# A fixed order for ScalarE's work in the attention start of a three-layer kernel, with a ring of its own for one set of tables

## The chip, the cores and the metric

The kernel runs on one core of a Trainium2 chip. What counts is the device time of one execution in microseconds; the time of a kernel is the median of its runs. A profile is one further execution, recorded by the hardware profiler, with a time of its own. The engines are TensorE (PE, its weight loads PEld), VectorE (DVE), ScalarE (ACT), GpSimd (POOL) and SyncE (SP), which here only issues DMAs. Each engine takes its instructions in the order of its queue.

## The reference

Three layers follow one another. The first is a linear attention with a decaying state, for 4 sequences, 8 heads, 768 steps and 64 columns a head:

```python
for t in range(S):
    state = gamma * state + einsum('bhd,bhe->bhde', k[:, :, t], v[:, :, t])
    y[:, :, t] = scale * einsum('bhd,bhde->bhe', q[:, :, t], state)
```

Its result is taken as 3072 tokens of 512 columns. The second layer is `h = x @ w_in` (512 to 2048), `g = h - tanh(h)`, `g @ w_out` (2048 to 512). The third is `h = x @ w_in` (512 to 1024), a softmax weighting `h * softmax(h)`, a layer norm with the gain `g_ln`, and `@ w_out` (1024 to 512). The weights of both come as 64-bit numbers. All of it is in float32; the kernel splits each operand of the large products into a high and a low part and takes three products for one.

## The kernel before

**Units.** The attention is cut into 6 chunks of 128 steps for each of 4 sequences: 24 units, four for each chunk c; unit k belongs to chunk k // 4. `unit(ko, ks)` (lines 237 to 309) does the output of unit `ko` and then the scores of unit `ks`. For the output: small products "out" of the state and of the masked scores on TensorE (line 207), copies of the results out of PSUM by ScalarE (lines 272 to 276; in chunk 0 there are three, later two), an addition on VectorE (line 278), and in `split_x` the high parts by ScalarE (line 316) and the low parts by VectorE or GpSimd (line 317). For the scores: products "sc" of k with q and of k with v (line 207), the mask on VectorE (line 298), and the running state `sb`, which ScalarE copies in chunk 0 (line 304) and VectorE adds later (line 306). An output needs the masked scores and `sb` of its unit. I write sc(k) and out(k) for the two sets of products: 64 matmuls for sc, 48 (chunk 0) or 64 for out.

**Before a unit.** `prepare(k)` (lines 210 to 235) scales q by a table on GpSimd (line 220) and v by a column of constants, on ScalarE head by head (line 227) and, for `own < H` heads, the rest on GpSimd (line 231). For units 0 to 7 ScalarE has four of the eight heads, and the results lie in tiles of the kind "vq"; for units 8 to 11 it has all eight.

**Weights.** A decoder takes a weight tile through four stages: load of the raw words (line 115), Abs on ScalarE (line 121), four operations on VectorE (lines 128 to 136), and the high part on ScalarE and low part on VectorE (lines 144 and 145). `dec1.to(st, n)` brings stage `st` up to weight n.

**Second layer.** A step (n, b) is `products_h(b, n)`, twelve matmuls of 128x512 (line 329), a tanh on ScalarE (line 335) and a subtraction on VectorE (line 336); b is the block of 512 tokens, n the weight. Steps (0,0) and (1,0) are traced among units 4 to 7, the other thirty in the loop over n behind them; that loop also traces units 8 to 11, one for each n from 3 to 7, behind the two steps of its n. The `w_out` products y for these two blocks follow ("y products", line 353), fed by splits gh and gl of the results (lines 341 and 344). Later blocks run step by step to 750 us, then comes the third layer.

**Memory.** Tiles of 4 KB a partition come from a pool of 44 ("t4"), those of 2 KB from a pool of 17 ("t2"); q's tables, one for each chunk, are t2 tiles too.

**Order.** A scheduler puts each engine's instructions in order by a timeline of its own. Instructions may so leave the order in which the program traces them, unless `keep_in_program_order` ties one behind the instruction traced before it on its engine. Before, only the products of line 207 are tied; the matmuls of line 329, ScalarE's work and the DMAs are not. SyncE issues all loads named here.

Of the kernel before, what the change touches and what calls it, by code (L numbers as in the profile page):

```python
# [26 lines left out]
F32 = mybir.dt.float32  # L27
# [8 lines left out]
B, H, S, D = 4, 8, 768, 64  # L36
P = 128
DM = H * D
NT = B * S
NP = H // 2  # L40
# [5 lines left out]
NF1, NF2, NK = FF1 // P, FF2 // P, DM // P  # L46
# [1 line left out]
LAG = 2  # L48
LATER = 3
LOADS = 3  # L50
N4, N2 = 44, 17


W_MIN, W_MAX = (
# [7 lines left out]
C_IDENT = C_MASK + D  # L62
# [28 lines left out]
def body(ctx: ExitStack, tc, z, w_in, w_out, w_in2, w_out2, g_ln, cst, tab, out):  # L91
    nc = tc.nc
# [3 lines left out]
    mid = ctx.enter_context(tc.tile_pool(name="mid", bufs=N2))  # L96
    stp = ctx.enter_context(tc.tile_pool(name="stp", bufs=B + 2))
    yd = ctx.enter_context(tc.tile_pool(name="yd", bufs=1, space=DRAM))

    def t4(shape, dtype, name):  # L100
        return big.tile(shape, dtype, tag="t4", name=name)

    def t2(shape, dtype, name):
        return mid.tile(shape, dtype, tag="t2", name=name)
# [76 lines left out]
    loaded = [0]  # L181

    def load_tab(c):
        tb[c] = t2([P, NP * P], F32, "tab")
        nc.sync.dma_start(out=tb[c], in_=tab[c])

    def load_half(k, half):
        t = t4([P, 2, NP, P], F32, "z")
# [12 lines left out]
    def rows(h):  # L201
        return slice(h * D, (h + 1) * D)

    def products(todo):
        for o, a, b in todo:
            tc.keep_in_program_order(
                nc.tensor.matmul(o, a, b, start=True, stop=True, skip_group_check=True)  # L207
            )

    def prepare(k, own, wide=False):  # L210

        c = k // B
        if wide:
            t = t4([P, 2, H * D], F32, "vq")
            v = t[:, 0, :].rearrange("q (h d) -> q h d", h=H)
            qs[k] = t[:, 1, :].rearrange("q (p t) -> q p t", p=NP)
        else:
            v = t2([P, H, D], F32, "vs")
            qs[k] = t2([P, NP, P], F32, "qs")
        nc.gpsimd.tensor_tensor(  # L220
            qs[k].rearrange("q p t -> q (p t)"),
            zq[k][:, 0, :, :].rearrange("q p t -> q (p t)"), tb[c], ALU.mult,
        )
        src = zv[k][:, 1, :, :].rearrange("q p (h d) -> q (p h) d", h=2)
        c0 = C_VS + c * H
        for h in range(own):
            nc.scalar.activation(  # L227
                v[:, h, :], src[:, h, :], AF.Copy, scale=con[:, c0 + h : c0 + h + 1]
            )
        if own < H:  # L230
            nc.gpsimd.tensor_tensor(
                v[:, own:, :], src[:, own:, :],
                con[:, c0 + own : c0 + H].unsqueeze(2).to_broadcast([P, H - own, D]), ALU.mult,
            )
        vs[k] = v

    def unit(ko, ks, hold=False, pool=ps_r, tag="r", engs=None):


        if ko is not None:  # L240
            c, b = divmod(ko, B)
# [27 lines left out]
            ya = [t.rearrange("q h i t -> q (h i) t") for t in y]  # L269
            if c:  # L270
                for h in range(2):
                    nc.scalar.copy(xf[:, h, :, :], fr[h])
            else:
                for h in range(2):
                    nc.scalar.copy(xf[:, h, :, rows(1)], fr[h][:, :, rows(1)])
                nc.scalar.copy(xa[:, :, rows(0)], ya[0])
            for ab in steps:
                nc.vector.tensor_tensor(
                    xa[:, :, rows(ab)], xa[:, :, rows(ab)], ya[ab], ALU.add
                )  # L280
            if not hold:
                split_x(c, b, xf, engs or (nc.gpsimd, nc.gpsimd))
        if ks is not None:
            c = ks // B
            kt, kv, v, q = zq.pop(ks)[:, 1, :, :], zv.pop(ks), vs[ks], qs[ks]
# [22 lines left out]
                sa[ks + B] = stp.tile([P, NP, D], F32, tag="sa", name="sa")  # L308
                nc.vector.tensor_tensor(sa[ks + B], sb[ks], gn[1], ALU.add)

    def split_x(c, b, xf, engs):
        if b == 0:
            xt[c] = [[t4([P, 2, SB], F32R, f"x{n}") for _ in range(2)] for n in "hl"]
        for h in range(2):
            xh, xl = (xt[c][n][h][:, :, b * P : (b + 1) * P] for n in range(2))
            nc.scalar.copy(xh, xf[:, h, :, :])
            engs[h].tensor_tensor(xl, xf[:, h, :, :], xh.bitcast(F32), ALU.subtract)  # L317


# [2 lines left out]
    def products_h(s, f, pool, tag):  # L322
        ph = pool.tile([P, SB], F32, tag=tag, name="ph")
        (ah, al) = (w.rearrange("p (k c) -> p k c", k=NK) for w in dec1.w[f])
        n = 0
        for k in range(NK):
            xh, xl = (xt[s][m][k // 2][:, k % 2, :] for m in range(2))
            for a, x in ((ah, xh), (ah, xl), (al, xh)):
                nc.tensor.matmul(ph, a[:, k, :], x, start=n == 0, stop=n == 3 * NK - 1)  # L329
                n += 1  # L330
        return ph

# [71 lines left out]

    load_half(0, 0)
    load_tab(0)
    nc.sync.dma_start(out=con, in_=cst[:, :C_IDENT])
    load_half(0, 1)
    loaded[0] = 1
    load_units(3)  # L410
# [1 line left out]
    load_units(6)  # L412
    dec1.to(0, 2)
    load_units(2 * B)
    prepare(0, H // 2, True)
    prepare(1, H // 2, True)
    unit(None, 0, **spare)
    prepare(2, H // 2, True)
    unit(None, 1, **spare)
    for k in range(2 * B):  # L420
        if k + 3 < 2 * B:
            prepare(k + 3, H // 2, True)
        both = (nc.vector, nc.gpsimd) if k < 2 * B - 1 else (nc.vector, nc.vector)
        unit(k, k + 2 if k + 2 < 2 * B else None, engs=both, **spare)

        if k in (1, 4):
            for st in (1, 2):
                dec1.to(st, 1 + (k > 1))
        elif k in (2, 5):
            dec1.to(3, 1 + (k > 2))  # L430
        if k in (4, 6):
            step_h((k - 4) // 2, 0)
    dec1.to(0, 4)
    nc.sync.dma_start(out=gl, in_=g_ln)
    for n in range(NF1):
        while dec1.at[3] < n + 1:
# [240 lines left out]
```

## Time and profile before

| | us |
|---|---|
| median of 3 runs | 920.63 |
| their spread | 919.2 to 920.88 |
| the profiled execution | 919.89 |
| its span, first to last instruction | 918.1 |
| TensorE busy in the span | 878.7 (96%) |
| VectorE, ScalarE, GpSimd busy | 432.4, 300.5, 192.3 |

The span is 1.79 us shorter than the time of the same execution. Busy time of TensorE holds pipelined matmuls whose ends are modelled, so a full stretch may still run at a lower clock; the granted clock of a stretch (1.00 is the upper of its two levels, 2.4 GHz, 0.50 the lower, 1.2 GHz) is read beside it. In the rows, "idle before <- releaser" tells what ended an engine's wait; "issue" means that nothing in the profile explains it. A row "x4" merges four like instructions.

### The profile page before, as it was taken

How to read it: one execution, taken by the hardware profiler on the slowest of the kernel's cores; microseconds unless marked ns; L12 is line 12 of the kernel's file. 1: busy time of each engine (PE TensorE's matmuls, PEld its weight loads, DVE VectorE, ACT ScalarE, POOL GpSimd, SP SyncE). 2: the span in 40 equal slices, each digit the busy share in tenths (PEclk: the TensorE clock that was granted, in tenths of full speed). 3: DMA queues.
4: the chain of work that ended last, by engine and by line, in shares of the span. 5: the costliest groups of instructions: out<-in, count | busy, mean ns of one | idle time of the engine just before them, and what ended most of it. 6: DMA issues, size and time to landing. Idle time of an engine off the chain costs nothing.

```text
span 918.1 us, 15885 instructions
## 1 busy us (share of the span) xinstructions
PE 878.7 (96%) x6656; PEld 725.5 (79%) x6656; DVE 432.4 (47%) x873; ACT 300.5 (33%) x606; POOL 192.3 (21%) x200
## 2 busy tenths in 40 slices
PE   3669899999999999999999999999999999999998
PEld 3558688788888887888878888888888888888886
DVE  1664886995132323222222249973644444444442
ACT  3444543663111111111111133532533333333332
POOL 3511000000034433333333310010211222222210
PEclk9799999999999999999999999999999999999999
DMA  9750211532311113001311026205111111000000
GB/s 359 291 216 26 86 32 35 194 92 92 87 63 47 54 58 132 10 39 58 93 46 48 24 84 199 85 11 152 33 46 46 46 46 47 24 24 24 24 24 35
DMA packets 34775, 71.93 MB, mean 78 GB/s; under 512 B 3088, under 2 KB 15504, under 8 KB 34704
## 3 DMA queue, kind: packets, MB, share of 16 engines
q1 hardware_dynamic: 18576, 58.33, 18.9%
q10 hardware_dynamic: 16128, 12.59, 4.3%
q8 instruction: 52, 0.85, 0.4%
q14 instruction: 19, 0.16, 0.0%
HBM read 58.32 MB, written 12.58 MB: 77 GB/s over the span
## 4 chain that ended last, share of the span: by engine, by line
PE 92%; DMA 3%; ACT 1%; DVE 1%; issue 1%; SPq 1%; POOL 1%; ACTq 0%; POOLq 0%; DVEq 0%
PE py L353 28%; PE ph L329 28%; PE po L601 14%; PE ph L553 14%; PE out L207 3%; PE sc L207 2%; PE ptr L588 2%; DMA z<-z 1%; DMA raw<-w_in 1%; DMA y1d<-ysb 1%; SPq L189 0%; ACT vq L227 0%; POOL qs L220 0%; DVE wf L135 0%; ACT th L335 0%
## 5 line engine op out<-in xcount | busy, mean ns | idle before, releaser
L329 PE MATMUL ph<-xh,w 128*128 128x512 f32 x768 | 250.2, 395 | 7.7 <-ACT w L144 5.5
L353 PE MATMUL py<-gh,w 128*128 128x512 f32 x768 | 248.9, 392 | 1.2 <-ACT gh L341 1.2
L329 PEld LDWEIGHTS ph<-xh,w 128*128 128x128 f32 x768 | 146.3, 191 | 39.5 <-ACT w L144 5.9
L353 PEld LDWEIGHTS py<-gh,w 128*128 128x128 f32 x768 | 143.4, 188 | 31.9 <-ACT gh L341 1.6
L336 DVE TENSOR_TENSOR g<-ph,th 128x512 f32<-128x512 f32 x96 | 66.2, 689 | 183.7 <-ACT th L335 180.5
L329 PE MATMUL ph<-xl,w 128*128 128x512 f32 x384 | 151.7, 395 | 0.3 <-DVE xl L317 0.3
L353 PE MATMUL py<-gl,w 128*128 128x512 f32 x384 | 149.8, 390 | 0.0
L335 ACT ACTIVATE th<-ph 128x512 f32<-128x512 f32 x96 | 57.1, 597 | 266.6 <-PE ph L329 251.0
L553 PE MATMUL ph<-w,y 128*128 128x512 f32 x576 | 134.9, 389 | 0.0
L344 POOL TENSOR_TENSOR gl<-g,gh 128x512 fp32r<-128x512 f32 x48 | 61.7, 1286 | 346.3 <-DVE gh L343 332.3
L553 PEld LDWEIGHTS ph<-w,y 128*128 128x128 f32 x576 | 108.0, 188 | 22.4
L601 PE MATMUL po<-w,uh 128*128 128x512 f32 x384 | 120.4, 395 | 0.0
L388 POOL TENSOR_TENSOR y<-yl,y 128x512 fp32r<-128x512 f32 x24 | 42.2, 1760 | 260.9 <-ACT y L387 260.9
L329 PEld LDWEIGHTS ph<-xl,w 128*128 128x128 f32 x384 | 73.4, 191 | 15.8 <-DVE xl L317 0.7
L559 DVE TENSOR_REDUCE nmx<-ph 128x1 f32<-128x1024 f32 x24 | 29.4, 1225 | 117.7 <-PE ph L553 117.7
L353 PEld LDWEIGHTS py<-gl,w 128*128 128x128 f32 x384 | 72.1, 188 | 14.9
L601 PEld LDWEIGHTS po<-w,uh 128*128 128x128 f32 x384 | 70.5, 188 | 13.6
L601 PE MATMUL po<-w,ul 128*128 128x512 f32 x192 | 75.3, 392 | 0.0
L562 ACT ACTIVATE ex<-ph,nmx 128x1024 f32<-128x1024 f32 x24 | 26.8, 1117 | 132.5 <-DVE nmx L559 132.5
L564 DVE SCALAR_TENSOR_TENSOR ex<-ph,ex 128x1024 f32<-128x1024 f32 x24 | 29.4, 1225 | 29.8 <-ACT ex L562 29.8
L601 PEld LDWEIGHTS po<-w,ul 128*128 128x128 f32 x192 | 36.0, 188 | 7.6
L298 DVE TENSOR_TENSOR pr<-sc,con 128x256 f32<-128x256 f32 x48 | 19.8, 419 | 44.4 <-PE sc L207 44.4
(76 smaller groups left out, 849.3 us busy)
## 6 DMA issues: line engine op xcount, KB each, us to landing
z<-z SPq DMA_DIRECT2D x48, 512.0 KB, 5.2
raw<-w_in SPq DMA_DIRECT2D x24, 512.0 KB, 4.3
raw<-w_out SPq DMA_DIRECT2D x24, 512.0 KB, 3.6
y1d<-ysb ACTq DMA_DIRECT2D x24, 256.0 KB, 3.7
yl<-y1d SPq DMA_DIRECT2D x24, 256.0 KB, 3.2
out<-ob ACTq DMA_DIRECT2D x24, 256.0 KB, 2.2
tab<-tab SPq DMA_DIRECT2D x6, 256.0 KB, 3.8
ident<-cst SPq DMA_DIRECT2D x1, 64.0 KB, 8.1
```

What stands on the lines that cost most here:

```text
L207: nc.tensor.matmul(o, a, b, start=True, stop=True, skip_group_check=True)
L329: nc.tensor.matmul(ph, a[:, k, :], x, start=n == 0, stop=n == 3 * NK - 1)
L335: nc.scalar.activation(th, ph, AF.Tanh)
L336: nc.vector.tensor_tensor(g, ph, th, ALU.subtract)
L344: eng_l.tensor_tensor(gl_, g, gh.bitcast(F32), ALU.subtract)
L353: nc.tensor.matmul(py[e], a[:, cols], x, start=f == 0 and n == 0, stop=f == NF1 - 1 and n == 2)
L388: nc.gpsimd.tensor_tensor(yo, t, yh.bitcast(F32), ALU.subtract)
L553: nc.tensor.matmul(ph[:, half, :], a[:, k, :], b, start=n == 0, stop=n == 3 * NK - 1)
L559: nc.vector.tensor_reduce(nmx, phf, AX.X, ALU.max, negate=True)
L562: nc.scalar.activation(ex, phf, AF.Exp, bias=nmx, scale=1.0, accum_out=ssum)
L564: nc.vector.scalar_tensor_tensor(ex, phf, 1.0, ex, ALU.mult, ALU.mult, accum_out=us)
L601: nc.tensor.matmul(po, a[:, f, :], b, start=n == 0, stop=n == 3 * NF2 - 1)
```

## The change

The change has five parts:

- A helper `pin` ties an instruction in program order when asked. For units 0 to 7 it ties ScalarE's copies out of PSUM, its v scaling (`prepare` with `wide`) and its high parts. `prepare(k + 3)` moves from ahead of `unit(k, k + 2)` into it, between the copies and the additions (`amid`). At the start, `prepare` and `unit` of units 0 and 1 alternate.
- The matmuls of line 329 are tied for the first two blocks (s < 2).
- q's tables get a ring of two buffers of their own; the t2 pool goes from 17 to 15.
- The first table and the constants are loaded by ScalarE's queue, no longer by SyncE's.
- Behind the units, three weights are brought through all four stages, where before only four loads stood.

```diff
-N4, N2 = 44, 17
+N4, N2 = 44, 15
...
+    def pin(ins, on=True):
+
+        if on:
+            tc.keep_in_program_order(ins)
...
     def load_tab(c):
-        tb[c] = t2([P, NP * P], F32, "tab")
-        nc.sync.dma_start(out=tb[c], in_=tab[c])
+        tb[c] = stp.tile([P, NP * P], F32, tag="tab", name="tab", bufs=2)
+        (nc.sync if c else nc.scalar).dma_start(out=tb[c], in_=tab[c])
...
         for h in range(own):
-            nc.scalar.activation(
+            pin(nc.scalar.activation(
                 v[:, h, :], src[:, h, :], AF.Copy, scale=con[:, c0 + h : c0 + h + 1]
-            )
+            ), wide)
...
             if c:
                 for h in range(2):
-                    nc.scalar.copy(xf[:, h, :, :], fr[h])
+                    pin(nc.scalar.copy(xf[:, h, :, :], fr[h]), amid)
             else:
                 for h in range(2):
-                    nc.scalar.copy(xf[:, h, :, rows(1)], fr[h][:, :, rows(1)])
-                nc.scalar.copy(xa[:, :, rows(0)], ya[0])
+                    pin(nc.scalar.copy(xf[:, h, :, rows(1)], fr[h][:, :, rows(1)]), amid)
+                pin(nc.scalar.copy(xa[:, :, rows(0)], ya[0]), amid)
+            if amid:
+                amid()
...
-            nc.scalar.copy(xh, xf[:, h, :, :])
+            pin(nc.scalar.copy(xh, xf[:, h, :, :]), fixed)
...
             for a, x in ((ah, xh), (ah, xl), (al, xh)):
-                nc.tensor.matmul(ph, a[:, k, :], x, start=n == 0, stop=n == 3 * NK - 1)
+                pin(
+                    nc.tensor.matmul(ph, a[:, k, :], x, start=n == 0, stop=n == 3 * NK - 1), s < 2
+                )
...
-    nc.sync.dma_start(out=con, in_=cst[:, :C_IDENT])
+    nc.scalar.dma_start(out=con, in_=cst[:, :C_IDENT])
...
-    prepare(0, H // 2, True)
-    prepare(1, H // 2, True)
-    unit(None, 0, **spare)
+    for k in range(2):
+        prepare(k, H // 2, True)
+        unit(None, k, **spare)
     prepare(2, H // 2, True)
-    unit(None, 1, **spare)
+
+    def ahead(k):
+        if k < 2 * B:
+            prepare(k, H // 2, True)
+
     for k in range(2 * B):
-        if k + 3 < 2 * B:
-            prepare(k + 3, H // 2, True)
         both = (nc.vector, nc.gpsimd) if k < 2 * B - 1 else (nc.vector, nc.vector)
-        unit(k, k + 2 if k + 2 < 2 * B else None, engs=both, **spare)
+        unit(
+            k, k + 2 if k + 2 < 2 * B else None, engs=both,
+            amid=lambda: ahead(k + 3), **spare
+        )
...
-    dec1.to(0, 4)
+    for st, n in enumerate((4, 3, 3, 3)):
+        dec1.to(st, n)
     nc.sync.dma_start(out=gl, in_=g_ln)
```

## Rows read from the trace of the kernel before

**Rows 1.** The page, engines: busy us (share of the span) and instructions.
```profile
PE 878.7 (96%) x6656; PEld 725.5 (79%) x6656; DVE 432.4 (47%) x873; ACT 300.5 (33%) x606; POOL 192.3 (21%) x200
```

**Rows 2.** Busy time by stretch: us, PE, PEld, DVE, ACT, POOL, clock, DMA share, GB/s.
```profile
0.00:41.60 41.60, 20.42 (x704) 18.87 (x704) 15.87 (x35) 18.05 (x62) 19.35 (x25) 0.86 0.93 358
41.60:50.00 8.40, 8.40 (x219) 7.01 (x214) 6.86 (x17) 4.30 (x11) 1.43 (x2) 0.86 0.02 4
...
66.74:72.00 5.26, 5.26 (x14) 4.16 (x15) 5.16 (x8) 1.14 (x2) 1.34 (x1) 0.57 0.34 100
92.10:98.40 6.30, 2.90 (x132) 2.53 (x129) 6.26 (x15) 4.44 (x14) 0.00 (x0) 1.00 0.56 168
98.40:103.00 4.60, 4.60 (x15) 3.66 (x14) 4.53 (x10) 2.58 (x10) 0.00 (x0) 0.63 0.01 2
120.00:200.00 80.00, 78.81 (x348) 64.91 (x348) 67.77 (x127) 42.67 (x79) 0.00 (x0) 1.00 0.28 91
```

**Rows 3.** TensorE in order of time: start us, us, what [idle before <- releaser].
```profile
10.85 1.99 PE L207 MATMUL sc<-vq,z 64*64 64x64 f32 x64 [0.54 <-POOL vq L220]
18.55 0.71 PE L207 MATMUL out<-vq,sb 64*64 64x64 f32 x16 [5.71 <-ACT sb L304]
...
26.32 0.28 PE L207 MATMUL sc<-vq,z 64*64 64x64 f32 x3 [2.09 <-issue]
...
32.49 0.28 PE L207 MATMUL out<-vq,sb 64*64 64x64 f32 x3 [2.90 <-issue]
...
38.77 0.38 PE L207 MATMUL out<-vq,sb 64*64 64x64 f32 x4 [0.99 <-issue]
...
54.91 0.73 PE L329 MATMUL ph<-xh,w 128*128 128x512 f32 x2 [2.15 <-ACT xh L316]
```

**Rows 4.** ScalarE in order of time.
```profile
17.18 1.06 ACT L227 ACTIVATE vq<-z,con 128x64 f32<-128x64 f32 x4 [2.78 <-DMA z<-z]
...
31.81 0.62 ACT L144 CAST w<-wf 128x512 fp32r<-128x512 f32 x1 [4.41 <-DVE wf L135]
...
60.13 0.60 ACT L335 ACTIVATE th<-ph 128x512 f32<-128x512 f32 x1 [4.96 <-PE ph L329]
60.63 1.77 ACT L121 ACTIVATE wf<-raw 128x512 f32<-128x512 f32 x3
...
66.07 1.22 ACT L144 CAST w<-wf 128x512 fp32r<-128x512 f32 x2 [3.19 <-DVE wf L135]
...
81.07 3.94 ACT L227 ACTIVATE vs<-z,con 128x64 f32<-128x64 f32 x16
```

**Rows 5.** The same columns as rows 2, between the ends of TensorE's "issue" waits.
```profile
26.30:32.40 6.10, 3.28 (x127) 3.18 (x127) 5.14 (x7) 1.31 (x4) 5.95 (x6) 0.72 1.04 398
32.40:38.70 6.30, 3.88 (x127) 3.12 (x126) 3.50 (x9) 4.55 (x19) 0.73 (x1) 0.60 1.03 406
```

**Rows 6.** DMA queues from 30.0 to 30.2 us: packets, MB, share of 16 engines.
```profile
q8 instruction: 1, 0.02, 33.9%
```

**Rows 7.** Waits of TensorE, 0 to 130 us: total, times, longest, in us.
```profile
PE ph L329 <- ACT w L144: 5.5, 1, 5.5
```

**Rows 8.** SyncE's queue in order of time: issue start us, us.
```profile
2.11 2.79 SPq L189 DMA_DIRECT2D z<-z  x5
...
29.46 2.51 SPq L189 DMA_DIRECT2D z<-z  x4
50.07 0.33 SPq L185 DMA_DIRECT2D tab<-tab  x1
```

**Rows 9.** Waits from 120 to 760 us: total, times, longest, in us.
```profile
ACT gh L341 <- PE py L353: 16.3, 11, 2.1
...
PE py L353 <- ACT gh L341: 1.2, 1, 1.2
```

**Rows 10.** Groups by line, 160 to 200 us: busy us, mean ns, idle before.
```profile
L344 DVE TENSOR_TENSOR gl<-g,gh 128x512 fp32r<-128x512 f32 x20 | 13.3, 678 | 0.0
L341 ACT CAST gh<-g 128x512 fp32r<-128x512 f32 x20 | 11.9, 618 | 2.0 <-PE py L353 2.0
```

More of the change, by code (lines that the diff above doesn't have):

```diff
@@ L205, in products @@
         for o, a, b in todo:
-            tc.keep_in_program_order(
-                nc.tensor.matmul(o, a, b, start=True, stop=True, skip_group_check=True)
-            )
+            pin(nc.tensor.matmul(o, a, b, start=True, stop=True, skip_group_check=True))
     def prepare(k, own, wide=False):
@@ L226, in prepare @@
         for h in range(own):
-            nc.scalar.activation(
+            pin(nc.scalar.activation(
                 v[:, h, :], src[:, h, :], AF.Copy, scale=con[:, c0 + h : c0 + h + 1]
-            )
+            ), wide)
         if own < H:
@@ L235, in prepare, with unit @@
         vs[k] = v
-    def unit(ko, ks, hold=False, pool=ps_r, tag="r", engs=None):
+    def unit(ko, ks, hold=False, pool=ps_r, tag="r", engs=None, amid=None):
         if ko is not None:
@@ L281, in unit @@
             if not hold:
-                split_x(c, b, xf, engs or (nc.gpsimd, nc.gpsimd))
+                split_x(c, b, xf, engs or (nc.gpsimd, nc.gpsimd), amid)
         if ks is not None:
@@ L309, in unit, with split_x @@
                 nc.vector.tensor_tensor(sa[ks + B], sb[ks], gn[1], ALU.add)
-    def split_x(c, b, xf, engs):
+    def split_x(c, b, xf, engs, fixed=False):
         if b == 0:
```

## Prediction

> **What bounds the kernel now.** I read the engines' busy time first, then stretches of the span, and only then single waits. TensorE is busy for 878.7 of 918.1 us [rows 1], so at most some 39 us of idle time and what a low clock costs are there to win. The stretches show where [rows 2]: from 120 to 200 us TensorE is idle for 1.2 us in 80, while up to 41.6 us it is idle for 21 us, and at 92.1 to 98.4 us for 3.4 us. In 66.74 to 72 us and in 98.4 to 103 us it is full, but its granted clock is 0.57 and 0.63: each time right behind a stretch in which it stood. So the change can act in the first 105 us only, which is also where its lines run.
>
> Four waits make up the part up to 67 us. First, out(0) begins at 18.55 us after 5.71 us of waiting for the copy sb of unit 0 [rows 3]. The products for it were done long before. ScalarE had the v scaling of units 1, 2 and 3 in front of the copy, and unit 3's data came only at 17.15 us [rows 4]. Second, three waits of 2.09, 2.90 and 0.99 us end at 26.32, 32.49 and 38.77 us with no releaser at all ("issue") [rows 3]. Between two of them stand 127 matmuls with 127 weight loads, both times [rows 5], and shortly before each end one packet of the instruction queue runs (one of three such windows is shown) [rows 6]. I read them as TensorE waiting for its next block of code, some 6.2 us a block (32.49 - 26.32 = 6.17, 38.77 - 32.49 = 6.28) while loads fill the DMA engines (share 0.93 up to 41.6 us [rows 2]). Third, 2.15 us before h step (0,1), for the high parts of unit 7 [rows 3]. Fourth, 5.5 us before h step (2,0) at 66.74 us, for the third decoded weight [rows 7]: ScalarE's Abs of that weight stands behind a tanh at 60.13 us, before which ScalarE was idle for 4.96 us [rows 4].
>
> **ScalarE in program order.** Nothing is added to the work; 32 v scalings, 20 copies and 16 high parts of units 0 to 7 change places. Per unit ScalarE now runs copies out of PSUM, v scaling of unit k + 3, high parts, sb. The wait for sb(0) goes: its input is there when sc(0) ends, ahead of sc(1), so out(0) can follow sc(1), which ends at 12.84 us [rows 3], in place of 18.55. What is late next is the code. Counted back by 127 matmuls from the first code wait, a block limit lies late in sc(2) and one early in sc(1). The first of these stays near 11 us, as the data of unit 1 set it; 6.2 us later, at about 17, the next may be passed, and TensorE is there by then, since it is 5.7 us earlier than before (about 21). From there each block of 127 matmuls (about one unit) takes 6.2 us as long as the loads run: limits at about 17, 23.2, 29.4 and 35.6 us, the last three in place of 26.3, 32.5 and 38.8. So of 5.65 us won at out(0), about 3.2 are left at the last of them (38.77 - 35.6).
>
> The order costs waits too. High parts of unit 0 now stand behind the scaling of unit 3, so until 17.15 + 1.06 = 18.2 us [rows 4]; out(2) needs sb(2) by 23.2 us, so that hides. The cast of the first weight stands before the copies of unit 3. ScalarE waited 4.41 us for that decode [rows 4]; started by 23.3 us it is over by 28.2, ahead of out(3), which the code holds to about 30 us. Without the code limit this would show, at up to 4.4 us.
>
> **The ring of its own for q's tables.** Before, the load of the third table stands at 50.07 us on SyncE, its predecessors having been issued by 32 us [rows 8], and the DMA engines lie idle from 41.6 to 50 us (share 0.02 [rows 2]). Two buffers for tables let it go at once, and the loads behind it with it: units 10 and 11 and four weights by the program's order, 4 x 0.52 + 4 x 0.52 + 0.26 = 4.5 MB, at the 358 GB/s of the first stretch some 12 us. Nobody waits for them before 66 us. But they keep the engines full until about 52 us, and so code slow for two blocks more. Quiet, the way from the last code wait to step (0,1) would be as before, 54.91 - 38.77 = 16.1 us, ending at 51.7. Loaded, blocks end at 41.8 and 48.0 us, and the rest of out(6), step (1,0), out(7) and the 2.15 us wait take some 6.3 us more: 54.3. The scratch tiles that the loads need decide it, and no row shows them; the loads behind the table went within 4 us of it, so I take 53.4, nearer to the loaded end. Gain 1.5 us (ends 0.6 and 3.2; I leave 1 us below nothing for a late ScalarE).
>
> The Trainium skill (Runtime: NRT & Kernel Launch, Instruction fetch mechanics) says that instructions come in 16 KiB blocks of 256, which fits 2 x 127, but also that crossing a block is mostly hidden. This trace agrees on the blocks and disagrees on the hiding while loads run: 5.98 us in three waits [rows 3]. By the page those waits would be about 0, which is the first rival below.
>
> **Table 0 and the constants on ScalarE's queue.** The second half of unit 0 is issued at 2.11 us [rows 8] after two issues of about 0.45 us that leave SyncE: up to 0.9 us earlier. The bytes ahead of it are the same, so 0 to 0.9; I take 0.3 and count nothing, as the code limit swallows it. If ScalarE issues them behind its table load, the table comes some 1.5 us later; that hides behind v of unit 0, which is there only after 8 us.
>
> **The third weight decoded ahead.** Three weights are taken through all stages before step (0,1) is traced, so the Abs is no longer behind its tanh. It adds no work. Two weights went from the first Abs at 60.63 us to the second cast at 67.29 us [rows 4], other work between them; one weight's share of that, 3 to 4 us, now lies beside unit 7 and steps (0,1) and (1,1), 6.3 us of products. Without that cover it costs its share. The 5.5 us wait goes, step (2,0) begins at 66.74 - 1.5 - 5.5 = 59.7 us, and the low clock behind the wait goes with it: 5.26 x (1 - 0.57) = 2.3 us [rows 2]. Next late is the fourth weight, cast some 7 us after the tanh of step (0,1) as the pair was before (60.13 to 67.29): with step (0,1) done by about 56.5, at 63.6. It is due at 59.7 + 5.5 = 65.2.
>
> **The h products pinned.** Before, units 8 to 11 had slipped behind step (5,1); sc(8), out(8) and sc(9) then stood together without work between them, and TensorE idled 3.4 us [rows 2]. In program order two h steps (5.5 us) stand between one unit's scores and its out products, so that wait goes, and the low clock behind it: 4.6 x (1 - 0.63) = 1.7 us. A new wait comes at sc(8): the v scaling of units 8 and 9 (16 ops, 3.94 us) follows the tanh of step (3,1) [rows 4], and nothing may pass it now: 0.6 + half of 3.94 less 0.9 for scores and drain = 1.7 us (0 if the scheduler puts the scaling into an idle ScalarE, 3.4 if unit 9 waits as well). Net 3.4 - 1.7 + 1.7 = 3.4 us.
>
> **Sum.** 1.5 + 5.5 + 2.3 + 3.4 = 12.7 us. The profiled execution took 919.89 us (1.79 around its span); the median of the three runs is 920.63, 0.74 above it. 919.89 - 12.7 + 0.74 = 907.9, say 908. By the ends of its terms this case reaches from 903 to 912.
>
> **Rivals.**
> 1. Code is hidden after all: TensorE no longer runs into the block limits, as the scheduler spreads the units otherwise or the fetch starts earlier. The three waits (5.98 us) go on top: 902, and with sc(8) free too, 900. For it: two blocks later, at quiet queues, no such wait shows. Against it: two equal blocks of 6.2 us under load.
> 2. The decode is not pinned, so the scheduler may put Abs of the third weight behind the tanh again: then 5.5 and 2.3 us stay, the change doesn't do there what it says, and 920.6 - 4.9 = 916 is left. For it: ScalarE was idle before that tanh, and the weight had been loaded, yet Abs wasn't put there before.
> 3. Nothing moves: new waits in ScalarE's fixed order (the 4.4 us of the first decode, late high parts) and at sc(8) eat the gain: 920.
> 4. Slower: scratch tiles t2 fall from 17 to 15. In the y products of the first two sequence blocks (from 161 us on) the third table is used up and the fourth not yet wanted, so two are truly lost there. ScalarE's splits gh already wait for y products to give tiles back, 16.3 us in 11 waits, so far beside a TensorE that waited 1.2 us [rows 9]. If two fewer make each of some 14 weights wait for one split (0.62 us on ScalarE, 0.68 on VectorE [rows 10]), that is 14 x 1.3 = 18 us: 908 + 18 = 926. It decides once more than 15 tiles are wanted at a time; I count 8 for two weights' splits and 4 in decode, so 12 or 13.
>
> **How the numbers follow.** Forecast 0.50, hidden code 0.15, decode unmoved 0.15, nothing 0.06, slower 0.14. The predicted time is the forecast's. A range from 898 to 918 takes in the first three cases with their bounds and leaves out 0.20. A measurement of this kernel tells about 0.2% (1.8 us) from no change; so faster 0.80, same 0.06, slower 0.14.
>
> **What would show it.** Right: out(0) near 13 us; sb(0) behind v of unit 0; code waits that end some 6.2 us apart and start earlier; the third table issued by 35 us; no wait at step (2,0), which begins before 61 us at full clock; sc(8) behind step (3,1). Wrong: no "issue" waits on TensorE (rival 1); Abs of the third weight behind the tanh of (0,1) (rival 2); TensorE waiting for gh in the y products (rival 4).

## Result and the profile after

The changed kernel takes 906.58 us (median of 4 runs, 906.52 to 906.91) against 920.75 us (919.2 to 921.09) of the kernel before on the same chip: a ratio of 0.985, 95% interval 0.9833 to 0.9867. The forecast was 908. The profiled execution took 906.58 us with a span of 904.8, so the span fell by 13.3 us. That of before lay 0.86 us below its median, that of after on it; so the medians differ by 14.2 us.

Line numbers have moved with the change: the unit products are line 211 (207 before), the v scaling 230 (227), the high parts 323 (316), the h products 337 (329), the tanh 344 (335). In the kernels that hold loads (below) they stand some 4 to 6 lines later again.

The page's engine line, which answers [rows 1]: TensorE's busy time fell by 3.0 us; the products are the same (x6656 both times), so I put this down to clock and pace; the rest of the 13.3 us was idle time.

```profile
PE 875.7 (97%) x6656; PEld 723.9 (80%) x6656; DVE 434.4 (48%) x873; ACT 301.5 (33%) x606; POOL 192.9 (21%) x200
```

Busy time by stretch of the changed kernel, with the columns of [rows 2]. The first five lines cut the start at h steps (0,0), (0,1), (2,0), (3,0) and at the end of unit 11; the last two are stretches of [rows 2].

```profile
0.00:35.50 35.50, 19.97 (x705) 18.48 (x705) 16.15 (x33) 17.58 (x62) 19.50 (x25) 0.86 0.89 335
35.50:53.52 18.02, 12.01 (x285) 9.69 (x281) 11.44 (x29) 7.55 (x20) 3.47 (x4) 0.89 1.03 409
53.52:59.66 6.14, 5.85 (x25) 4.61 (x25) 5.42 (x10) 2.99 (x6) 1.62 (x1) 1.00 0.18 71
59.66:65.10 5.44, 5.44 (x26) 4.50 (x24) 5.44 (x12) 2.37 (x5) 0.00 (x0) 1.00 0.00 0
65.10:104.10 39.00, 38.13 (x633) 31.15 (x631) 32.21 (x67) 22.58 (x63) 2.68 (x2) 1.00 0.27 89
...
92.10:98.40 6.30, 6.30 (x147) 5.24 (x146) 5.04 (x12) 2.93 (x6) 0.00 (x0) 1.00 0.02 4
98.40:103.00 4.60, 4.60 (x21) 3.57 (x19) 4.53 (x12) 1.11 (x2) 0.00 (x0) 1.00 0.42 118
```

From 53.5 us on TensorE is nearly full and its granted clock is 1.00. The two low stretches of before (0.57 and 0.63) have no counterpart. What is left stands ahead of 53.5 us: 21.5 of these 53.5 us are idle, and the granted clock of the first two stretches is 0.86 and 0.89.

The waits of TensorE in that part, from its timeline (start, duration, operation; in brackets the idle time before and what ended it), against [rows 3]:

```profile
11.54 0.31 PE L211 MATMUL out<-vq,sb 64*64 64x64 f32 x1
...
15.76 0.51 PE L211 MATMUL sc<-vq,z 64*64 64x64 f32 x18 [1.61 <-issue]
21.81 0.28 PE L211 MATMUL sc<-vq,z 64*64 64x64 f32 x3 [3.00 <-issue]
28.00 0.28 PE L211 MATMUL out<-vq,sb 64*64 64x64 f32 x4 [2.83 <-issue]
...
44.81 0.34 PE L211 MATMUL out<-vq,sb 64*64 64x64 f32 x8 [3.99 <-issue]
...
53.52 0.50 PE L337 MATMUL ph<-xh,w 128*128 128x512 f32 x1 [2.02 <-ACT xh L323]
```

The 5.71 us wait for sb is gone; out(0) begins at 11.54 us. Three "issue" waits end 6.05 and 6.19 us apart. The first has no counterpart, as TensorE then still stood for sb; the other two end 4.5 us earlier than before (21.81 for 26.32, 28.00 for 32.49). For the one at 38.77 there is none near 34 us, and a new one of 3.99 us ends at 44.81.

Set against the trace of before, by starts of the same products:

| stretch | before | after | gain | term of the sum |
|---|---|---|---|---|
| start to step (0,1) | 54.91 | 53.52 | 1.4 | 1.5 |
| (0,1) to (2,0) | 11.83 | 6.14 | 5.7 | 5.5 |
| (2,0) to (2,1) | 4.93 | 2.72 | 2.2 | 2.3 |
| (2,1) to the h step behind out(11) | 45.30 | 41.79 | 3.5 | 3.4 |
| from there to the end of the span | 801.1 | 800.6 | 0.5 | 0 |

ScalarE's timeline against [rows 4]: the copy sb of unit 0 stands ahead of v scaling, and Abs (line 126) and cast (line 149) of the third weight stand ahead of the tanh (line 344) of step (0,1).

```profile
9.66 0.37 ACT L311 COPY sb<-sc 128x256 f32<-128x256 f32 x1 [1.45 <-DVE pr L305]
9.93 1.06 ACT L230 ACTIVATE vq<-z,con 128x64 f32<-128x64 f32 x4
...
52.07 0.68 ACT L126 ACTIVATE wf<-raw 128x512 f32<-128x512 f32 x1
...
56.92 0.62 ACT L149 CAST w<-wf 128x512 fp32r<-128x512 f32 x1 [3.15 <-DVE wf L140]
57.45 0.59 ACT L344 ACTIVATE th<-ph 128x512 f32<-128x512 f32 x1
```

SyncE's timeline against [rows 8]: the third and the fourth table (one merged row, from 23.06 to 29.9 us), and behind them the weights.

```profile
23.06 6.83 SPq L190 DMA_DIRECT2D tab<-tab  x2
29.94 3.75 SPq L120 DMA_DIRECT2D raw<-w_in  x6
```

The scores of unit 8 stand behind step (3,1), as foreseen, with a wait of 0.88 us in their middle; the next h step follows at 74.14 us:

```profile
70.63 0.69 PE L211 MATMUL sc<-qs,z 64*64 64x64 f32 x32
72.20 2.01 PE L211 MATMUL sc<-vs,z 64*64 64x64 f32 x32 [0.88 <-ACT vs L230]
```

### The profile page after: what moved, and what is told of

It is laid out like the page before. It is cut to its first block, busy times and chain, and to the rows that moved or that the text cites. A ratio compares the mean times of both kernels' runs of the same rounds, so it can differ in the third digit from the quotient of the medians.

```text
span 904.8 us, 15888 instructions
## 1 busy us (share of the span) xinstructions
PE 875.7 (97%) x6656; PEld 723.9 (80%) x6656; DVE 434.4 (48%) x873; ACT 301.5 (33%) x606; POOL 192.9 (21%) x200
## 4 chain that ended last, share of the span: by engine, by line
PE 93%; DMA 3%; DVE 1%; issue 1%; ACT 1%; POOL 1%; SPq 0%; POOLq 0%; ACTq 0%
PE ph L337 29%; PE py L362 29%; PE po L616 15%; PE ph L568 14%; PE ptr L603 2%; PE out L211 2%; PE sc L211 2%; DMA z<-z 2%; DMA y1d<-ysb 1%; POOL qs L223 0%; DVE xl L324 0%; POOL vs L234 0%; DVE wf L140 0%; DVE w L150 0%; ACT th L344 0%
## 5 line engine op out<-in xcount | busy, mean ns | idle before, releaser
L362 PEld LDWEIGHTS py<-gh,w 128*128 128x128 f32 x768 | 143.4, 188 | 31.8 <-ACT gh L350 1.6
L397 POOL TENSOR_TENSOR y<-yl,y 128x512 fp32r<-128x512 f32 x24 | 42.2, 1760 | 260.9 <-ACT y L396 232.5
L574 DVE TENSOR_REDUCE nmx<-ph 128x1 f32<-128x1024 f32 x24 | 29.4, 1225 | 117.7 <-PE ph L568 117.7
L579 DVE SCALAR_TENSOR_TENSOR ex<-ph,ex 128x1024 f32<-128x1024 f32 x24 | 29.4, 1225 | 29.8 <-ACT ex L577 29.8
L149 ACT CAST w<-wf 128x512 fp32r<-128x512 f32 x48 | 29.6, 618 | 29.6 <-DVE wf L140 29.4
```

Source lines behind the costliest of these rows:

```text
L149: nc.scalar.copy(hi, wf)
L362: nc.tensor.matmul(py[e], a[:, cols], x, start=f == 0 and n == 0, stop=f == NF1 - 1 and n == 2)
L397: nc.gpsimd.tensor_tensor(yo, t, yh.bitcast(F32), ALU.subtract)
L574: nc.vector.tensor_reduce(nmx, phf, AX.X, ALU.max, negate=True)
L579: nc.vector.scalar_tensor_tensor(ex, phf, 1.0, ex, ALU.mult, ALU.mult, accum_out=us)
```

## The experiments

All runs, with the ratio to the kernel before on the same chip:

| run | median us (lowest to highest) | ratio, 95% interval |
|---|---|---|
| the change | 906.58 (906.52 to 906.91) | 0.9850 (0.9833 to 0.9867) |
| e1_no_decode_ahead | 913.09 (912.96 to 913.34) | 0.9918 (0.9902 to 0.9935) |
| e2_no_pin_h | 909.33 (909.15 to 909.72) | 0.9877 (0.9862 to 0.9892) |
| e3_no_scalar_order | 913.00 (910.57 to 914.51) | 0.9914 (0.9892 to 0.9936) |
| e4_tables_in_t2 | 905.96 (903.34 to 907.83) | 0.9838 (0.9816 to 0.9859) |
| e5_loads_held | 905.24 (904.14 to 907.64) | 0.9832 (0.9813 to 0.9851) |
| e6_table0_on_sync | 908.37 (907.58 to 910.96) | 0.9867 (0.9848 to 0.9886) |
| e7_eleven_scratch_tiles | 907.47 (906.18 to 908.29) | 0.9856 (0.9839 to 0.9872) |
| e8_held_and_filled | 901.73 (901.51 to 903.16) | 0.9794 (0.9779 to 0.9808) |
| e9_held_short | 904.16 (903.63 to 904.53) | 0.9818 (0.9800 to 0.9836) |
| e10_table4_not_ahead | 909.46 (908.77 to 909.84) | 0.9873 (0.9857 to 0.9889) |
| e11_before_with_ring | 918.23 (916.68 to 919.97) | 0.9972 (0.9961 to 0.9982) |
| e12_held_filled_short | 905.42 (903.27 to 906.97) | 0.9825 (0.9801 to 0.9849) |

The runs of e3 to e7 and e12 lie up to 4.5 us apart, those of the change within 0.4. The runs were made on several chips, on which the median of the kernel before is 920.42 to 921.26 us; differences to the change are given between medians, and by the ratios they can come out up to 0.8 us otherwise. Where medians differ by less than 2 us, the verdicts below rest on the trace.

**The decode ahead.** The decode line alone is undone.

```diff
-    for st, n in enumerate((4, 3, 3, 3)):
-        dec1.to(st, n)
+    dec1.to(0, 4)
```

> The changed kernel with one part undone: behind the units only four loads stand again, the third weight is no longer decoded ahead. Theory: this part alone took away the wait before step (2,0) and the low clock behind it, 5.5 + 2.3 us, so it comes back: about 914 us (913 to 915), with the Abs of the third weight behind the tanh of step (0,1). Rival (the decode would have been hidden anyway once ScalarE is in order): 906.6 us, no wait at step (2,0).

913.09 us, 6.5 more than the change. Step (2,0) in this kernel's timeline of TensorE, then the stretch of that step in this kernel, then the same step in the changed kernel (us, busy time of PE, PEld, DVE, ACT, POOL, clock, DMA share, GB/s):

```profile
63.65 0.79 PE L337 MATMUL ph<-xh,w 128*128 128x512 f32 x1 [3.94 <-ACT w L149]
```
```profile
63.65:69.24 5.59, 5.59 (x12) 3.97 (x13) 4.45 (x8) 1.14 (x2) 0.00 (x0) 0.50 0.00 0
```
```profile
59.66:62.38 2.72, 2.72 (x14) 2.25 (x12) 2.72 (x7) 0.67 (x2) 0.00 (x0) 1.00 0.00 0
```

The wait for the third weight is back with 3.94 us, and behind it the granted clock is 0.50, the lower level, and the step takes 2.87 us more. Together 6.8 us; 0.6 us of it comes back at sc(8), where the wait falls from 0.88 to 0.30. So this one line, which adds no work, is nearly half of the gain.

**The pin of the h products.** Its condition is replaced by `False`.

```diff
-                    nc.tensor.matmul(ph, ...), s < 2
+                    nc.tensor.matmul(ph, ...), False
```

> The changed kernel with the h products of the first two blocks no longer tied in program order. Theory: units 8 to 11 slip behind step (5,1) again, the 3.4 us of idle time between sc(8), out(8) and sc(9) and the low clock behind it (1.7) come back, the wait of 0.9 us at sc(8) goes: +4.2 us, about 910.8. Rival (the slip came from late inputs, which the other parts have cured): 906.6 us and sc(8) behind step (3,1) also without the tie.

909.33 us, 2.75 more, where 4.2 was expected. The scores of unit 8 slip to 80.37 us, behind step (5,1), as before the change, and sc(8), out(8), sc(9) follow one another from 80.37 to 84.9 us with only 1.3 us of h products between them, inside out(8). TensorE is full up to there; the next out has this wait, and the stretch from step (5,1) on a clock of 0.91:

```profile
87.69 0.33 PE L211 MATMUL out<-qs,sa 64*64 64x64 f32 x2 [2.09 <-DVE xc L285]
```
```profile
78.69:97.00 18.31, 16.22 (x356) 12.63 (x355) 13.61 (x31) 8.72 (x27) 1.40 (x1) 0.91 0.47 159
```

So the other parts don't cure the slip; in this kernel the pin keeps the units between the h steps. Less comes back than expected: one wait of 2.09 us, where before lost 3.4 us [rows 2].

**ScalarE's order.** The pins of its copies, scaling and high parts are off, and `prepare` stands where it stood; the ring, the first table's queue, the h pins and the decode stay.

```diff
-            ), wide)
+            ), False)
...
+        ahead(k + 3)
         unit(
             k, k + 2 if k + 2 < 2 * B else None, engs=both,
-            amid=lambda: ahead(k + 3), **spare
+            **spare
```

> The changed kernel with ScalarE's part undone: prepare stands ahead of each unit again and ScalarE's copies, v scaling and high parts of units 0 to 7 are not tied. Theory (code blocks limit the start): out(0) falls back from 11.5 to about 17 us, but the blocks of 6.2 us swallow part of it: +2 to +4 us, 908.5 to 910.5. Rival A (ScalarE's order is the main source of the gain): +6 us or more, above 912.5. Rival B (the code swallows all): 906.6.

913.0 us: 6.4 more, where the main theory had 2 to 4 more, so rival A is borne out. The profiled run (914.09) is one of the slower ones; the fastest took 910.57, 4.0 more. TensorE's timeline:

```profile
18.74 0.71 PE L211 MATMUL out<-vq,sb 64*64 64x64 f32 x16 [7.11 <-ACT sb L311]
...
49.67 0.38 PE L211 MATMUL out<-vq,sb 64*64 64x64 f32 x3 [3.05 <-issue]
```

The wait for sb is back, and step (0,1) begins at 59.61 us: 6.1 later than with the change and 4.7 later than before it. So the parts don't add up: ScalarE's order is worth some 6 us beside the ring, and the ring without it makes step (0,1) later (the next run has it alone).

**The ring alone.** The kernel before, with nothing but the ring of two and 15 scratch tiles.

```diff
-N4, N2 = 44, 17
+N4, N2 = 44, 15
...
-        tb[c] = t2([P, NP * P], F32, "tab")
+        tb[c] = stp.tile([P, NP * P], F32, tag="tab", name="tab", bufs=2)
```

> The kernel before with one part of the change alone: the ring of two for q's tables and 15 scratch tiles. Theory (loads that are let go keep code slow): the queues stay full from 41.6 to some 55 us, code waits come at about 45 and 51 us, step (0,1) begins at 57 to 58 in place of 54.9: slower by 2 to 4 us, 923 to 925. Rival (the loads are hidden, as nothing waits for them): 920.7; or the earlier weights help: faster.

918.23 us, 2.2 less than before: the expected 923 to 925 is missed on its far side. TensorE's timeline, and the stretch from sc(8) to out(9):

```profile
50.67 0.28 PE L207 MATMUL out<-vq,sb 64*64 64x64 f32 x3 [4.05 <-issue]
...
59.33 0.73 PE L329 MATMUL ph<-xh,w 128*128 128x512 f32 x2 [2.02 <-ACT xh L316]
70.59 0.80 PE L329 MATMUL ph<-xh,w 128*128 128x512 f32 x1 [5.53 <-ACT w L144]
```
```profile
90.57:102.47 11.90, 11.86 (x230) 9.61 (x229) 9.44 (x21) 6.79 (x22) 1.40 (x1) 1.00 0.43 153
```

The first part did what the theory said: a code wait at loaded queues at 50.67, step (0,1) 4.4 us late, step (2,0) 3.9 late. What it left out came later: with the loads of units 9 to 11 issued before 50 us, an h step stands between sc(8) at 90.57, sc(9) at 96.95 and out(9) at 102.47, and TensorE idles for 0.04 us in these 11.9 us, where before it lost 3.4 us and clock [rows 2]. So the ring has a second effect, which the pin of the h products has as well. That would explain why it is worth nothing more beside that pin.

**The ring left out of the change.** Tables go back to the scratch tiles, 17 of them; all else stays.

```diff
-N4, N2 = 44, 15
+N4, N2 = 44, 17
...
-        tb[c] = stp.tile([P, NP * P], F32, tag="tab", name="tab", bufs=2)
+        tb[c] = t2([P, NP * P], F32, "tab")
```

> The changed kernel with q's tables back in the t2 pool, which has 17 tiles again. Theory: the fourth table no longer stands in front of the weights on SyncE at 29.6 us; the third stands there later and holds the loads behind it, so the DMA engines fall idle between 41 and 50 us and the code wait of 3.99 us that ends at 44.8 us shrinks or goes: 2 to 4 us faster, 902.5 to 904.5. Rival (the loads behind the table don't matter, the wait is no code wait): 906.6 us with the wait in place; if the own ring was needed for its own sake, slower.

905.96 us, where 902.5 to 904.5 was expected; the runs spread from 903.34 to 907.83 and can't be told from the change. The trace is of the fastest run. In it step (0,1) starts at 50.34 us, 3.2 earlier. The stretches 30 to 35 and 40 to 45 us, first of this kernel, then of the change (columns as in [rows 2]):

```profile
30.00:35.00 5.00, 2.53 (x87) 2.15 (x83) 3.62 (x12) 3.07 (x12) 2.06 (x3) 0.50 1.02 403
...
40.00:45.00 5.00, 5.00 (x202) 4.32 (x201) 4.30 (x9) 2.88 (x8) 0.28 (x1) 1.00 0.01 3
```
```profile
30.00:35.00 5.00, 4.14 (x145) 3.95 (x144) 3.62 (x12) 3.87 (x16) 2.01 (x3) 0.50 0.81 252
...
40.00:45.00 5.00, 1.01 (x68) 0.88 (x63) 4.39 (x10) 1.88 (x5) 0.72 (x1) 1.00 1.03 409
```

With the third table waiting for a scratch tile (issued at 44.20 us) the DMA engines fall silent, share 0.01 from 40 to 45 us, and TensorE does 202 matmuls there without a gap. In the change the DMA share is 1.03 there, and TensorE works for 1.01 us of 5. But at 30 to 35 us the change is ahead, 4.14 us of work against 2.53: there its share is 0.81, and this kernel has a code wait of 1.65 us ending at 34.48.

**The fourth table held back.** The hole in the loads about 30 us (DMA share 0.25 from 28 to 30 us) was not in the forecast. SyncE issued the fourth table at 29.56 us, when the ring gave it a buffer, ahead of the weights in the program: it held them up. Here the tables are tied in program order behind the loads traced before them.

```diff
-        (nc.sync if c else nc.scalar).dma_start(out=tb[c], in_=tab[c])
+        pin((nc.sync if c else nc.scalar).dma_start(out=tb[c], in_=tab[c]), c > 1)
```

> The changed kernel with the third and fourth table tied in program order on SyncE, so that neither runs ahead of the weights; the loads are not held. Theory (what matters is that queues are full while the code of units 6 and 7 is fetched): 17 loads still follow the units without a gap, to about 52 us, the code wait near 44 us stays at 3 to 4 us and step (0,1) near 53: 906 to 907 us. Rival (the fourth table in front of the weights was the loss that e4 took away): 903 to 904.5 us.

909.46 us, 2.9 slower (2.1 by the ratios), where 906 to 907 was expected. The stretch 30 to 35 us and TensorE's waits in this kernel:

```profile
30.00:35.00 5.00, 2.37 (x106) 2.05 (x102) 3.61 (x11) 2.98 (x11) 1.89 (x3) 0.81 1.03 409
```
```profile
34.38 0.21 PE L211 MATMUL out<-vq,sa 64*64 64x64 f32 x1 [1.97 <-issue]
46.51 0.49 PE L211 MATMUL out<-vq,sb 64*64 64x64 f32 x8 [3.72 <-issue]
```

Without the hole the code wait near 34 us is there, and step (0,1) begins at 56.28 us, 2.8 later. The packets of the instruction queue (as in [rows 6]) show why: the one that begins at 25.4 us in the change is followed by the next after 3.6 us (29.0), in e1, e2 and e6, which have the hole too, after 3.6 to 4.2 us, but here after 6.2 us (25.6 and 31.8). So the change owes some 2 to 3 us to a fourth table that stops the weights by accident, just when TensorE wants its next block of code.

**Loads held until the units are through.** If loads make code slow, holding those behind unit 9 until the scores of unit 7 are done must take the wait at 44.8 us away. GpSimd copies a column of the masked scores of unit 7 into a small tile, and a copy of that tile on SyncE stands in program order ahead of them.

```diff
+            if ks == 2 * B - 1:
+                pin(nc.gpsimd.tensor_copy(gate, pr[:, 0, 0, 0:1]))
...
+    held[0] = True
     for st, n in enumerate((4, 3, 3, 3)):
         dec1.to(st, n)
...
+    pin(nc.sync.dma_start(out=gate_d, in_=gate))
```

While `held[0]` is true, every load of a weight or a unit is tied behind that copy; so are the tables from the third on.

> The changed kernel with the loads behind the first four weights held: on SyncE a load-queue copy of one column of a tile that is written when sc(7) is masked stands in front of weights 5 and up, units 8 to 11 and the third table, and the loads behind it are tied in program order (the fourth table can't run ahead either). Theory (TensorE waits for code while loads run): the queues are quiet from about 33 to 43 us, so the code wait of 3.99 us that ends at 44.8 us goes; step (0,1) begins at 49 to 50.5 us in place of 53.5, 902 to 903.5 us. Rival (the wait has another cause, such as PSUM or ScalarE's order): step (0,1) stays at 53.5 and the time at 906.6; or the held loads come too late and the steps from 60 us on wait for weights: above 907.

905.24 us; 902 to 903.5 was expected. The stretch from 35 to 45 us, and step (0,1):

```profile
35.00:45.00 10.00, 10.00 (x253) 8.22 (x252) 8.79 (x23) 5.05 (x15) 1.66 (x4) 0.93 0.02 4
```
```profile
48.97 0.49 PE L343 MATMUL ph<-xh,w 128*128 128x512 f32 x1 [3.04 <-ACT xh L329]
```

The mechanism holds: at a DMA share of 0.02 TensorE does 253 matmuls, two blocks of code, without a gap, and step (0,1) starts 4.55 us earlier than in the change. Most of that is given back: the small copy took 8.4 us from issue to landing, so the held loads begin late. From 45 to 53.8 us the clock is 0.81, the weights of steps behind 59 us come late (waits of 0.89 and 0.42 us), and sc(8) waits 1.01 us.

**The first table's queue.** The first table and the constants go back to SyncE.

```diff
-        (nc.sync if c else nc.scalar).dma_start(out=tb[c], in_=tab[c])
+        nc.sync.dma_start(out=tb[c], in_=tab[c])
...
-    nc.scalar.dma_start(out=con, in_=cst[:, :C_IDENT])
+    nc.sync.dma_start(out=con, in_=cst[:, :C_IDENT])
```

> The changed kernel with table 0 and the constants loaded by SyncE again, in the order of before. The second half of unit 0 then lands at about 8.2 us in place of 6.7. Theory (as the prediction put it: the code limit swallows it): 0 to +0.3 us, 906.6 to 906.9. Rival (the first block limit in sc(1) moves with the data of units 0 and 1, and every later one with it): +1.3 us, 907.9.

908.37 us, 1.8 more than the change; all its runs lie above all of the change's, though the intervals of the ratios overlap. The trace says more:

```profile
16.93 0.51 PE L211 MATMUL sc<-vq,z 64*64 64x64 f32 x18 [1.48 <-issue]
23.02 0.38 PE L211 MATMUL sc<-vq,z 64*64 64x64 f32 x3 [3.97 <-issue]
29.28 0.28 PE L211 MATMUL out<-vq,sb 64*64 64x64 f32 x4 [2.78 <-issue]
```

Each of the three code waits ends 1.2 to 1.3 us later than in the change, as does step (0,1) (54.77 for 53.52); in the other kernels that load the table by ScalarE and keep its order they end up to 0.6 us later than in the change, so at least half of the shift is the table's. The rival is right: the chain of blocks starts when the first units start, and all of it shifts. Two more waits, of 0.99 us at 33.77 and 1.16 at 39.98, come although the hole is there. The profiled run was the slowest of the four; its other losses, behind step (0,1), are not explained.

**Fewer scratch tiles.** Rival 4 of the prediction needs a price: 11 tiles in place of 15.

```diff
-N4, N2 = 44, 15
+N4, N2 = 44, 11
```

> The changed kernel with 11 scratch tiles t2 in place of 15. Theory (12 or 13 are wanted at a time in the y products): TensorE waits for splits gh there, 4 us or more in all, above 910.5. Rival (the scheduler uses tiles beyond 11 only to run ahead): within 1 us of 906.6.

907.47 us, not told from the change. Waits of TensorE in this kernel, then ScalarE's group of splits from 120 to 760 us, first here, then in the change (busy us, mean ns, idle time before and what ended it):

```profile
PE py L362 <- ACT gh L350: 1.3, 1, 1.3
```
```profile
L350 ACT CAST gh<-g 128x512 fp32r<-128x512 f32 x32 | 19.4, 618 | 21.3 <-PE py L362 20.5 <-DVE w L150 0.8
```
```profile
L350 ACT CAST gh<-g 128x512 fp32r<-128x512 f32 x32 | 19.2, 622 | 16.4 <-PE py L362 15.0 <-DVE w L150 1.2
```

ScalarE waits 5.5 us more for tiles, TensorE 0.1 us more. The splits run ahead as far as tiles allow; four tiles fewer shorten that lead, and TensorE hardly notices.

**A version beyond the change.** e5 left two gaps, and this one fills them: step (1,0) is moved behind unit 7, beside the wait for its high parts; the third weight is loaded and decoded beside units 6 and 7; and v of unit 8 is scaled one step earlier.

```diff
+    held[0] = True
+    dec1.to(0, 3)
...
+        elif k == 6:
+            for st in (1, 2):
+                dec1.to(st, 3)
+        elif k == 7:
+            dec1.to(3, 3)
-        if k in (4, 6):
+        if k in (4, 7):
...
+        if n == LATER - 1:
+            load_units(2 * B + 1)
+            prepare(2 * B, H)
...
```

> The kernel of e5 with three more steps: step (1,0) stands behind out(7) in place of out(6), so that its 2.75 us lie in the 2.0 us wait for unit 7's high parts; the third weight is loaded and decoded beside units 6 and 7; the v scaling of unit 8 is traced one step earlier, ahead of sc(8) by two h steps. Theory: 2.0 us at step (0,1) and 0.9 us at sc(8) on top of e5: 899 to 900.5. Rival (these waits hide nothing, other waits take their place): as e5.

901.73 us: 4.9 less than the change, ratio 0.9794 to the kernel before; 1.2 us above what was expected. Step (0,1), the scores of unit 8, and the stretch from step (0,1) to the end of unit 11:

```profile
51.18 0.50 PE L343 MATMUL ph<-xh,w 128*128 128x512 f32 x1 [1.14 <-ACT xh L329]
...
67.95 0.69 PE L215 MATMUL sc<-qs,z 64*64 64x64 f32 x32
...
69.05 0.50 PE L343 MATMUL ph<-xh,w 128*128 128x512 f32 x1
```
```profile
51.20:98.90 47.70, 47.70 (x680) 39.07 (x680) 42.29 (x83) 28.29 (x72) 6.29 (x4) 1.00 0.64 233
```

From 51.2 to 98.9 us TensorE never stands and never loses clock. The scores of unit 8 take 1.10 us where the change takes 3.51 (70.63 to 74.14).

Two attempts to better it lost. e9 puts step (1,0) behind unit 6 and lets the gate copy 64 bytes of one partition:

```diff
-                pin(nc.gpsimd.tensor_copy(gate, pr[:, 0, 0, 0:1]))
+                pin(nc.gpsimd.tensor_copy(gate, pr[0:1, 0, 0, 0:16]))
...
-        if k in (4, 7):
+        if k in (4, 6):
```

> As e8, with two differences: step (1,0) stands behind out(6) again, and the copy that holds the loads moves 64 bytes of one partition in place of 4 bytes of each of 128 (that one took 8.6 us from issue to landing in e8, so that the fifth weight landed at 56.1 us). Theory: held loads land from about 48 us on, step (0,1) begins near 49 as in e5, no step waits for a weight, no wait at sc(8): 898.5 to 900.5 us. Rival (the waits of e5 behind step (0,1) came from VectorE, not from late loads): 901.5 or above.

904.16 us, 2.4 more than e8. The loads do begin earlier (270 GB/s from 45 to 50 us, 43 in e8), but step (0,1) gains nothing by it:

```profile
51.24 0.79 PE L343 MATMUL ph<-xh,w 128*128 128x512 f32 x1 [4.72 <-ACT xh L329]
```

In ScalarE's fixed order the third weight's cast (48.69 us, after 1.27 us of waiting for VectorE) stands ahead of the copies of out(7), whose products ended at 46.5 us.

e12 is e8 with the short gate copy and the decode of the third weight behind the units again, as in the change:

> The kernel of e8_held_and_filled (loads behind unit 9 held until sc(7), step (1,0) behind out(7), v of unit 8 scaled one step earlier) with two edits: the copies that hold the loads move 64 bytes of one partition in place of 4 bytes of 128 partitions, so the held loads start some 6 us earlier (near 48.6 us, as in e9_held_short), and the decode of the third weight is traced behind the units again, as in the change, and not beside units 6 and 7. Theory: in e8 unit 7's high parts waited 1.1 us and VectorE delayed out(7) by 1.4 us because the third weight's decode stood beside them; with the decode behind, step (1,0) begins near 45 us, step (0,1) at 48 to 49.5 us (e8: 51.18) without a long wait, and its decode is done within steps (1,0) to (1,1); 899 to 900.5 us. Rival: the decode moved behind unit 7 comes too late now that step (2,0) is due near 53.5 us: TensorE waits 1 to 3 us for the third weight there and the gain ahead of it is given back, 901.5 us or more.

905.42 us (903.27 to 906.97; the profiled run is the slowest): the rival is right. Step (2,0) in TensorE's timeline, and the stretch behind its first wait:

```profile
57.81 0.50 PE L343 MATMUL ph<-xh,w 128*128 128x512 f32 x1 [2.70 <-ACT w L153]
60.19 1.22 PE L343 MATMUL ph<-xh,w 128*128 128x512 f32 x2 [1.65 <-DVE w L154]
```
```profile
57.81:64.62 6.81, 5.16 (x13) 3.76 (x14) 6.66 (x11) 2.82 (x5) 1.17 (x1) 0.57 1.03 411
```

Step (0,1) starts at 49.48 without a long wait, 1.7 us before e8. But then step (2,0) is due before the third weight, and the wait brings the clock down to 0.57. The third weight must be decoded beside the units when the units are faster.

This trace also bounds the account of the code waits. Two "issue" waits, of 0.65 and 0.80 us, end at 32.85 and 40.74 us although the loads are held; the second, with the stretch ahead of it:

```profile
40.74 0.34 PE L215 MATMUL out<-vq,sb 64*64 64x64 f32 x8 [0.80 <-issue]
```
```profile
38.00:40.74 2.74, 1.94 (x133) 1.80 (x125) 2.67 (x6) 0.77 (x2) 0.00 (x0) 1.00 0.00 0
```

So quiet queues make these waits short or take them away; they don't rule them out.

## Why the prediction was right, and where not

**The terms.** Three of the four came out by their own mechanism. The wait at step (2,0) went (5.7 us for 5.5), step (2,0) began at 59.66 us (59.7), and the clock behind it gave 2.2 us (2.3); e1 shows both come from the decode line. Units 8 to 11 gave 3.5 us (3.4); without the pin 2.75 us are lost again (e2). There the price of the new wait was too low: sc(8) waits 0.88 us, but its second half then follows the v scaling head by head, 2.01 us for 32 products in place of 0.65. Against e8's 1.10 us the scores lose 2.4 us, not 1.7, and the rest of the stretch gains that much more.

**The first part** gave 1.4 us for 1.5, but not by the steps that I wrote. The wait for sb went, out(0) came at 11.54 us (13), and code waits about 6.1 us apart followed, as foreseen. Three steps failed:
- "I take 0.3 and count nothing, as the code limit swallows it" (the first table's queue). The limits are not fixed in time: they follow the start of the units. e6 puts this at 1.2 to 1.3 us at each of the first three limits: with the table back on SyncE they end at 16.93, 23.02 and 29.28 us, within 0.2 us of the predicted 17, 23.2 and 29.4, and with the change at 15.76, 21.81 and 28.00.
- The limit at 35.6 us did not come. The fourth table waited for a buffer of the ring until 29.56 us and held up the weights that SyncE had behind it; I had not seen that, and e10 prices it at 2.8 us at step (0,1), in favour of the change.
- "Loaded, blocks end at 41.8 and 48.0 us": one block ended at 44.81, with a wait of 3.99 us, longer than any of before. e4 and e5 show that without loads it isn't there, and in e5 step (0,1) comes 4.55 us earlier.

The errors cancel roughly: 1.2 us and 3 us to the good, about 4 us to the bad. So the size of the first part was right by luck. Its direction was not: e3 loses 6.4 us without ScalarE's order, four times the term, since the term held the ring's cost as well. (The 5.65 us that the prediction wins at out(0) are 18.55 - 12.84 = 5.71; no term uses them.)

**The rivals.** Hidden code: refuted where loads run, as the trace has three waits of 7.4 us up to 28 us, and one of 3.99 later; right in e4 and e5 where they don't, and nearly so in e12 (0.65 and 0.80 us). The Trainium skill (Runtime: NRT & Kernel Launch, Instruction fetch mechanics) has crossings mostly hidden; the runs agree at a DMA share of 0.01 to 0.02 in e4 and e5, and disagree near 1.0, and a little even at 0.00 (e12).

That a block of code is what TensorE waits for was a reading of the rows; the kept traces bear it out. The page of the change counts the packets of the instruction queue (packets, MB, share of 16 engines):

```profile
q8 instruction: 52, 0.85, 0.4%
```

TensorE has 6656 matmuls and 6656 weight loads, together 13312, which is 52 x 256. And up to 57 us all 55 "issue" waits of TensorE in the fourteen traces end 2.4 to 2.9 us behind the start of one of these packets (found in windows of 0.2 us), whatever the length of the wait: in the change 15.76, 21.81, 28.00 and 44.81 us behind packets at 13.2, 19.2, 25.4 and 42.2. Beside loads a packet begins late: 6.0 to 6.2 us after the one before it up to 25.4 us in the change, 3.4 to 4.6 us with the loads held (e5, 29.8 to 41.4 us). Why a packet begins later beside loads stays open.

Decode unmoved: refuted, Abs stands at 52.07 us, ahead of the tanh. Nothing moves: refuted by the time; of the waits that it named, the one at sc(8) came (0.88 us), and the one for the first decode (ScalarE waits 3.80 us, to 27.87) lies beside the code wait that ends at 28.00. Fewer scratch tiles: TensorE still waits 1.2 us for gh. The count of 12 or 13 tiles was wrong as a limit, since 11 do as well (e7).

**The last 1.4 us** between 908 and 906.58: 0.7 because the median was put above the profiled run as before, and after's is not; 0.5 behind unit 11; 0.1 in the terms; the rest is rounding.

**Open.** Why the runs of some versions spread by 3 to 4.5 us while the change's agree within 0.4; why a packet of code begins later beside loads; where the 0.5 us behind unit 11 come from; and whether e8 with the short gate alone, step (1,0) staying behind unit 7, beats 901.7.

## What to carry to other kernels

When two waits follow the same full queue, price the parts of a change together: ScalarE's order was worth 6 us with the loads let go early. Letting the loads go early made step (0,1) 4.4 us later on its own, won 2.2 us in all by what it did further on (e11), and was worth nothing that the runs can tell beside the other parts (e4). A load that nobody awaits wasn't free while TensorE ran through many small instructions: look at "issue" waits against the DMA share and the packets of the instruction queue, and try holding the loads back. And where TensorE waits a few us for one operand, look a step further for the clock behind the wait: here it cost 2 to 3 us on top.

## What the runs showed of the hardware

- "Issue" waits of TensorE depend on the load: 1.4 to 4.0 us where they come among 64x64 matmuls at a DMA share of 1.02 to 1.04 during the wait (the change, e10), none at 0.01 to 0.02 in e4 (40 to 45 us) and e5 (35 to 45 us), 0.65 and 0.80 us at 0.00 in e12.
- Each of these waits ended 2.4 to 2.9 us behind the start of a packet of the instruction queue (55 waits in fourteen traces). There are 52 such packets for 13312 matmuls and weight loads.
- A copy of 0.5 KB that is spread over 128 partitions, 4 bytes each, took 8.4 us from issue to landing (e5; 8.6 in e8), issued on quiet queues (share 0.02) and followed by loads.
- The granted clock was 0.50 in the step behind a wait of 3.94 us (e1), and 0.57 from 57.81 to 64.62 us behind a wait of 2.70 us, with one of 1.65 us inside (e12); after the 2.02 us wait at step (0,1) it was 1.00 (the change, 53.52 to 59.66 us).
